# Sharing rows between VectorE and TensorE anew, and moving zero-writes, on the way back of a two-layer decode block

## The chip, the core and the metric

The kernel runs on one core of one Trainium2 chip. The metric is the device time of one execution in microseconds (us), given as the median of several runs. Profiles come from one further execution, taken by the hardware profiler.

## The reference

One token (a row of D = 1024 values) passes through four blocks, A, B, A, B, each added to its input after a layer norm. A is attention of 32 heads over the last 4096 positions of a cache with 4 key/value heads; B is a two-layer perceptron of width F = 3584 with the activation h * tanh(softplus(h)). The same weights serve both layers. Wanted are the output and the gradients with respect to the input, the caches and all weights:

```python
def _A_ref(x, k_cache, v_cache, wq, wo):
    q = (x @ wq).reshape(B, Sq, Hq, Dh).transpose(0, 2, 1, 3)
    k = jnp.repeat(k_cache[:, :, Sk - W:, :], rep, axis=1)      # W = 4096 of Sk = 32768
    v = jnp.repeat(v_cache[:, :, Sk - W:, :], rep, axis=1)
    p = softmax(einsum("bhqd,bhkd->bhqk", q, k) * Dh ** -0.5)
    o = einsum("bhqk,bhkd->bhqd", p, v)
    return o.transpose(0, 2, 1, 3).reshape(B, Sq, Hq * Dh) @ wo
def _B_ref(x, w1, b1, w2):
    h = x @ w1 + b1
    return (h * tanh(softplus(h))) @ w2
x = A_x
for _ in range(2):
    x = x + _A_ref(layernorm(x), k_cache, v_cache, wq, wo)
    x = x + _B_ref(layernorm(x), w1, b1, w2)
out, vjp = jax.vjp(f, A_x, k_cache, v_cache, wq, wo, w1, b1, w2)
return (out, *vjp(grad_out))
```

Only the last 4096 of 32768 positions of the caches have a gradient; the other seven eighths of both cache gradients are zeros, and they have to be written: 56 pieces of 1 MiB.

## The kernel before

**Work.** All is bf16, one token wide, so nearly everything is a matrix times a vector. Weights come in chunks of 1 MiB. The way forward goes through A0, B0, A1, B1; the way back through B1, A1, B0, A0; then the weight gradients, outer products of rows kept from both layers, are formed in PSUM (with a K of 2 or 32), copied to SBUF as bf16 and stored.

**Loads.** `Ring` has 8 slots. All loads stand in one list in the order of their use and go out on SyncE's queue; the next goes out when a slot is released (`release` calls `pump`, L68), which happens when the last reader of a chunk is done. Three chunks of wq (`KEEP_Q2`) stay in the ring between layer 1 and layer 0 of the way back, already turned. VS, KT and w1 have places of their own.

**Zeros.** `zeros(n, after)` takes the next n of the 56 pieces and issues them on GpSimd's queue (L248). If `after` is given, a copy of one element of that tile stands ahead of them (L243), so that they go out when the tile is there. The calls are placed by hand all along the program.

**The way back.** A gradient g is needed against the weights' other side, so a chunk's products can be made in two ways. VectorE takes a row of 1024 (`rowdot`, L422): it multiplies it with the gradient, broadcast over the partitions in PSUM (`bcast`, L325), and sums. Or TensorE turns eight blocks of 128 (`turned`, L445), ScalarE or VectorE copies them back over the ring slot (`evac_t`, L298 or L301, picked by a tally `load` of each engine's planned time), and TensorE multiplies them with the gradient's columns (`mv`, L457). These products are held back behind some later transposes (`later`, `behind`). In `attn_bwd` the tables `NR_O[l][c]` and `NR_Q[t]` say how many of a chunk's four rows go to VectorE; the rest is TensorE's. The w2 loop for layer 0 (L1103) gives two of four to each, and beside that TensorE finishes the forward product of layer 1 with the same chunk (`mlp_out`, L667).

In order of time after the forward pass: dh1; `dn_b1` (w1, resident) gives g3; `attn_bwd(1, ...)`: the wo loop (hook `do`, with pieces of KT and VS turned beside it by `conv`, L596), the softmax's way back (L868 to L900, hook `dp`), the wq loop (hooks `dq` and `dn`), and `ln_bwd` (L386) gives g2; the w2 loop gives dh0; `dn_b0` (L821) gives g1; `attn_bwd(0, ...)` gives g0; then `work` forms what is left of the weight gradients. `ln_bwd` calls its argument `beside` twice, ahead of and behind the matmul at L401; layer 0 passes `units_a0` there, layer 1 nothing.

**w1's last blocks.** `dn_b1` turns most of w1 in place. Blocks 4 to 7 of each of the eight parts are turned later, by `w1_rest` (L777, transposes at L783), since `dn_b0` reads them turned: two in hook `dp`, two in `dq`, four in `dn`.

**PSUM** has eight banks: SC (two, also LB, the broadcast rows), MV, TP, three BIG that transposes go through, and one that is free.

Of the kernel before, what the change touches and what calls it, by code (L numbers as in the profile page):

```python
# [83 lines left out]
def kernel(  # L84
# [65 lines left out]

    SC = [psum.tile([P, 512], FP32, name=f"SC{i}")[:] for i in range(2)]
    MV = psum.tile([P, 512], FP32, name="MV")
    TP = psum.tile([P, 512], FP32, name="TP")
    bigs = [psum.tile([P, 512], FP32, name=f"BIG{i}")[:] for i in range(3)]
    big_n = [0]
# [119 lines left out]
    def even():  # L275
        load["D"] = load["A"] = max(load.values())
# [138 lines left out]
    def rowdot(w, vecs, n, acc, fours=False):  # L415

        for i, vec in enumerate(vecs):
            out, a = junk[:, 0:n], w[:, i * n:(i + 1) * n]
            if fours:
                out, vec = (x.rearrange("a (k p) -> a k p", p=P) for x in (out, vec))  # L420
                a = a.rearrange("a (p k) -> a k p", k=4)
            nc.vector.tensor_tensor_reduce(out=out, in0=a, in1=vec, scale=1.0,  # L422
                                           scalar=acc if i else 0.0, op0=ALU.mult, op1=ALU.add, accum_out=acc)
        load["D"] += len(vecs) * (n * 1.1e-3 + 0.18)
# [4 lines left out]
    def later(f, product=False):  # L429

        lag.append((product, f))
        while sum(p for p, _ in lag) > behind[0]:
            lag.popleft()[1]()
        while lag and not lag[0][0]:
            lag.popleft()[1]()
# [5 lines left out]
    def turned(w, n, mv, eng=None, block=None):  # L441

        b = big().bitcast(BF16)
        for i in range(n):
            nc.tensor.transpose(b[:, i * P:(i + 1) * P], block(w, i) if block else w[:, i * P:(i + 1) * P], ident_bf[:])  # L445
        evac_t(w, b[:, 0:n * P], eng)
        later(mv, True)

    fresh = [False]

# [385 lines left out]

    NR_O = {1: (0, 3, 3, 3, 2, 2, 2, 2), 0: (0, 2, 2, 2, 2, 2, 2, 2)}
    NR_Q = (0, 2, 2, 2, 2, 1, 1, 1)  # L840

    def attn_bwd(l, sv, g, wo_key, wq_key, wq_keep, hooks, beside=None):
        name = f"A{l}"
        nc.vector.tensor_copy(GA[:, :, l], g[:])
        bcast(lambda c: GA[:, c, l:l + 1], TD)
        do32 = tmp([P, HQ], FP32, "da")
        mv_open()
        even()
        for c in range(8):
            ch = ring.get((*wo_key, c))  # L850

            behind[0] = max(2, 6 - c)
            rows_chunk(ch, c, GA, l, LB[0], do32, DA, NR_O[l][c], None)
            later(lambda c=c: ring.release((*wo_key, c)))
            hooks["do"](c)
        flush()
        x = 0
        while x < 8:
            k0, n0 = NR_O[l][x], x
            while n0 < 8 and NR_O[l][n0] == k0:  # L860
                n0 += 1
            nc.vector.tensor_copy(do32[:, 4 * x:4 * n0].rearrange("p (c k) -> p c k", k=4)[:, :, k0:],
                                  TP[:, DA + 4 * x:DA + 4 * n0].rearrange("p (c k) -> p c k", k=4)[:, :, k0:])
            x = n0
        do_n = from_fours(do32[:])
        dov = DOC[:].rearrange("p v (g u l h) -> p v g u l h", g=G, u=2, l=2)
        do4 = do_n.rearrange("p (g h) -> p g h", g=G)
        nc.vector.tensor_copy(dov[:, 0, :, 0, l, :], do4)  # L868
        nc.gpsimd.tensor_copy(dov[:, 1, :, 1, l, :], dov[:, 0, :, 0, l, :])
        pr = small[:, 64:128]  # L870
        prv = pr[:].rearrange("p (g u h) -> p g u h", g=G, u=2)
        o4 = sv["o32"][:].rearrange("p (g h) -> p g h", g=G)
        for u in range(2):
            nc.vector.scalar_tensor_tensor(out=prv[:, :, u, :], in0=do4, scalar=float(D), in1=o4, op0=ALU.mult, op1=ALU.mult)
        sdp = small[:, 224:288]
        pxv = PX[:].rearrange("p (b l h) -> p b l h", l=2, h=8)
        dsv = DSX[:].rearrange("p (b l h) -> p b l h", l=2, h=8)
        for i in range(2):
            for t in range(16 * i, 16 * i + 16):
                for g_ in range(G):  # L880
                    c = scol(g_, t) - 512 * i
                    nc.tensor.matmul(SC[i][:, c:c + 8], lhsT=VS[:, g_, t, :],  # L882
                                     rhs=DOC[:, 0, g_ * 32 + l * 8:g_ * 32 + l * 8 + 8], start=True, stop=True)
            if i == 0:
                nc.tensor.matmul(TP[:, 320:384], lhsT=onesD[:], rhs=pr[:], start=True, stop=True)
                nc.vector.tensor_copy(sdp[:], TP[:, 320:384])
            s = SC[i].rearrange("p (tp c) -> p tp c", c=64)
            nc.vector.tensor_tensor(out=s, in0=s, in1=sdp[:, None, :].to_broadcast([P, 8, 64]), op=ALU.subtract)
            nc.vector.tensor_tensor(out=dsv[:, i * 64:(i + 1) * 64, l, :], in0=SC[i].rearrange("p (b h) -> p b h", h=8),
                                    in1=pxv[:, i * 64:(i + 1) * 64, l, :], op=ALU.mult)  # L890
        even()
        hooks["dp"]()
        dq_ps = MV[:, 320:320 + HQ]
        for i in range(2):
            for g_ in range(G):
                for t in range(16 * i, 16 * i + 16):
                    c = pcol(g_, t, l)
                    nc.tensor.matmul(dq_ps[:, g_ * 8:g_ * 8 + 8], lhsT=KT[:, g_, t, :], rhs=DSX[:, c:c + 8],  # L898
                                     start=(g_ == 0 and t == 0), stop=(t == TS - 1), skip_group_check=True)
        nc.vector.tensor_scalar(out=DQC[:, :, l], in0=dq_ps, scalar1=scale, scalar2=None, op0=ALU.mult)  # L900
        bcast(lambda c: DQC[:, c, l:l + 1], TD)
        even()
        hooks["dq"]()
        mv_open()
        nc.vector.memset(dnp[:, 0:1], 0.0)
        for t in range(TD):
            key = (*wq_key, t)
            ch = ring.get(key)
            nr = NR_Q[t]
            behind[0] = max(2, 6 - t)  # L910
            if nr:
                rowdot(ch[:, 0:nr * D], LB[0:nr], D, dnp[:, t:t + 1])
            for k in range(nr, 4):
                h0 = 8 * k
                w = ch[:, h0 * P:(h0 + 8) * P]
                f = lambda w=w, h0=h0, t=t, k=k: mv(w, 8, TP[:, t:t + 1], lambda i: DQC[:, h0 + i, l:l + 1], k == 3)
                if key in turned_q:
                    later(f, True)
                else:
                    turned(w, 8, f)  # L920
            if t == 0:
                bcast(lambda c: DQC[:, c, l:l + 1], 2 * TD, None, TD)
            if t in wq_keep:
                ring.keep(key, ("q", 3, t))
                turned_q.add(("q", 3, t))
            else:
                later(lambda key=key: ring.release(key))
            hooks["dn"](t)
        flush()
        return ln_bwd(dnp, sv["n32"], sv["rstd"], g, name, beside)  # L930
# [3 lines left out]

    nc.vector.tensor_tensor(out=dh1[:], in0=da1[:, 0:TF], in1=mp1[:], op=ALU.mult)
    nc.vector.tensor_copy(DHC[:, :, 1], dh1[:])
    zeros(8, dh1)
    g3 = dn_b1(g4)
    sB1["act_late"]()
    put_by("AC", AC, TF)  # L940
    zeros(4, g3)

    def dp3():
        w1_rest(2)
        zeros(4)

    def dq3():
        w1_rest(2)
        zeros(3, DQC[:, 0, 1:2])

    def dn3(t):
        if t % 2:
            w1_rest(1)
        if t == 5:
            zeros(1, dnp[:, t:t + 1])

    assert all(NR_Q[t] == (1 if t in KEEP_Q2 else 2) for t in range(1, 8))
    g2 = attn_bwd(1, sA1, g3, ("o", 1), ("q", 2), KEEP_Q2,
                  dict(do=lambda c: conv(2), dp=dp3, dq=dq3, dn=dn3))


    W1S = W1[:].rearrange("p t f -> p (t f)")
# [131 lines left out]


    nc.vector.tensor_copy(GB[:, :, 0], g2[:])
    zeros(3, g2)
    bcast(lambda c: GB[:, c, 0:1], TD)
    da0 = tmp([P, HQ], FP32, "da")
    y_ps = MV[:, 384:384 + TD]  # L1100
# [2 lines left out]
    for c in range(7):  # L1103
        ch = ring.get(("2", 1, c))
        mlp_out(1, ch, c, y_ps)
        rows_chunk(ch, c, GB, 0, LB[0], da0, DA)
        later(lambda c=c: ring.release(("2", 1, c)))
    flush()
    rows_join(da0, TF, DA)
    nc.vector.tensor_tensor(out=dh0[:], in0=da0[:, 0:TF], in1=mp0[:], op=ALU.mult)  # L1110
    nc.vector.tensor_copy(DHC[:, :, 0], dh0[:])
    w1_rest(len(w1_units))
    zeros(2, dh0)
    g1 = dn_b0(g2)
    nc.vector.tensor_copy(GA[:, :, 0], g1[:])
    zeros(2, g1)

    x4 = sb([P, TD], BF16, "x4")
    nc.vector.tensor_tensor(out=x4[:], in0=y_ps, in1=x3[:], op=ALU.add)
# [41 lines left out]
        work(4)  # L1161

    g0 = attn_bwd(0, sA0, g1, ("o", 3), ("q", 3), (), dict(do=do1, dp=dp1, dq=dq1, dn=dn1), units_a0)
    g0b = sb([P, TD], BF16, "g0b")
    nc.vector.tensor_copy(g0b[:], g0[:])
    store_rows(g0b[:], TD, out_1[0, 0, :])
# [46 lines left out]
```

## Time and profile before

| | |
|---|---|
| median of 3 runs | 459.95 us (458.6 to 460.88) |
| the profiled execution | 460.51 us, of which span 458.4 us |
| TensorE (matmul) busy | 315.7 us, 69% |
| VectorE busy | 262.3 us, 57% |
| ScalarE busy | 185.6 us, 40% |
| DMA | 183.53 MB, mean 400 GB/s |
| loads and stores (queue q1) | 123.94 MB |
| zeros (queue q0) | 58.72 MB |

Stages of the way back in the profiled execution, in us from the start of the span: dh1 at 167.3, g3 at 187.5, wo loop of layer 1 to 215, its wq loop from 226 to 247.8, g2 at 249.6, w2 loop to 280.2, dh0 at 280.7, g1 at 292.3, layer 0's wo loop to 315.6 and wq loop to 346, then stores to 458.4.

How to read the profile: the span is cut into 40 slices of 11.5 us; each digit is a busy share in tenths, PEclk the granted TensorE clock, GB/s what the DMA engines moved. Tables of windows give, for a stretch from A to B, busy time and number of instructions of each engine (PE TensorE's matmuls, PEld its weight loads, DVE VectorE, ACT ScalarE, POOL GpSimd), then the granted clock, the DMA engines' busy share and GB/s. A timeline line has start, duration, engine, line of the kernel, operation, output<-input, shape and count; brackets hold the idle time before it and what ended it. A queue's line has packets, MB and its share of 16 engines' time.

### The profile page before, as it was taken

To read this page: it belongs to the slowest core of one execution; us is meant where nothing else is said; L and a number is where in the kernel's file an instruction comes from. 1 tells how busy PE (TensorE), PEld (TensorE's weight loads), DVE (VectorE), ACT (ScalarE), POOL (GpSimd) and SP (SyncE) were. 2 spreads that over 40 slices of the span, in tenths; PEclk is the share of its full clock that TensorE was granted. 3 is DMA by queue.
4 is the path that set the end of the run, shared out by engine and by line. 5 is a ranking of instruction groups with operands and counts; after the bars stand their busy time and mean duration, and the time that the engine had idled before them with its cause. 6 is when DMAs were issued, how large, how long until landed. Compare 5 with 4: busy or idle time off the path is not lost. (4 is left out here: it accounts for less than half of the span.)

```text
span 458.4 us, 13440 instructions
## 1 busy us (share of the span) xinstructions
PE 315.7 (69%) x5965; PEld 257.1 (56%) x5965; DVE 262.3 (57%) x514; ACT 185.6 (40%) x288; POOL 38.4 (8%) x85
## 2 busy tenths in 40 slices
PE   3836435597678799791797858667964776667870
PEld 3835434496668799691796857567861121122440
DVE  7305731283060148498378746397396987878770
ACT  2402001034032358390064321152255987888770
POOL 4000000000102321101202001102111000000000
PEclk9955555555555569795588555595585555555555
DMA  8999999999999999999999998879999999999996
GB/s 336 422 420 420 419 419 417 420 402 345 401 422 425 420 416 415 412 401 424 414 422 422 420 398 277 365 270 406 423 421 423 419 424 425 423 424 419 407 409 250
DMA packets 28375, 183.53 MB, mean 400 GB/s; under 512 B 3706, under 2 KB 3734, under 8 KB 9494
## 3 DMA queue, kind: packets, MB, share of 16 engines
q1 hardware_dynamic: 20162, 123.94, 66.5%
q0 software_dynamic: 8064, 58.72, 30.9%
q8 instruction: 46, 0.75, 0.6%
q14 instruction: 11, 0.09, 0.1%
q10 hardware_dynamic: 92, 0.02, 0.0%
HBM read 83.94 MB, written 98.62 MB: 398 GB/s over the span
## 5 line engine op out<-in xcount | busy, mean ns | idle before, releaser
L422 DVE CUSTOM_DVE_ANT_0 junk<-ring,SC 128x1024 bf16<-128x1024 bf16 x59 | 72.0, 1220 | 13.1 <-DMA ring<-in_B_w_dram 10.3
L301 ACT COPY ring<-BIG 128x512 f32<-128x512 f32 x82 | 47.7, 586 | 63.5 <-PE BIG L445 56.0
L445 PE MATMUL BIG<-ident_bf,ring 128*128 128x128 bf16 x720 | 69.8, 262 | 3.9 <-DMA ring<-in_A_wo_dram 3.6
L1021 PE MATMUL wide<-W 2*128 2x512 bf16 x228 | 48.9, 603 | 19.3 <-DVE VS L284 4.9
L445 PEld LDWEIGHTS <-ring 128*128 128x128 bf16 x720 | 56.5, 119 | 4.8 <-DMA ring<-in_A_wo_dram 4.0
L1021 PEld LDWEIGHTS <-W 2*128 2x128 bf16 x240 | 10.4, 103 | 52.2 <-issue 51.5
L284 DVE CAST ring<-wide 128x1024 bf16<-128x1024 f32 x27 | 31.6, 1217 | 6.4 <-PE wide L1021 3.8
L287 ACT CAST ring<-wide 128x1024 bf16<-128x1024 f32 (+1 forms) x37 | 33.6, 986 | 4.0 <-PE wide L1021 3.6
L457 PEld LDWEIGHTS <-ring 128*128 128x128 bf16 x792 | 30.3, 102 | 2.7 <-ACT ring L301 2.7
L248 POOL DMA_DIRECT2D out_dram<-zt x56 | 29.6, 534 | 7.2 <-DMA out_dram<-zt 6.4
L301 ACT COPY KT<-BIG 128x512 f32<-128x512 f32 x25 | 14.2, 584 | 38.8 <-PE BIG L596 35.6
L567 PE MATMUL MV<-OC,ring 128*128 128x1 bf16 x512 | 16.6, 166 | 15.0 <-DMA ring<-in_A_wo_dram 12.4
L567 PEld LDWEIGHTS <-ring 128*128 128x128 bf16 x512 | 16.0, 105 | 15.8 <-DMA ring<-in_A_wo_dram 13.0
L487 PE MATMUL MV<-NA,ring 128*128 128x1 bf16 x512 | 15.2, 165 | 12.5 <-DMA ring<-in_A_wq_dram 12.5
L301 ACT COPY W<-BIG 128x512 f32<-128x512 f32 (+1 forms) x29 | 13.5, 495 | 25.3 <-PE BIG L783 23.2
L615 PE MATMUL MV<-NB,W 128*128 128x1 bf16 x448 | 16.3, 172 | 9.3 <-DMA W<-in_B_w_dram 6.5
L422 DVE CUSTOM_DVE_ANT_0 junk<-ring,DSX 128x1024 bf16<-128x1024 bf16 x18 | 22.0, 1224 | 0.6
L284 DVE CAST VS<-wide 128x1024 bf16<-128x1024 f32 (+1 forms) x17 | 19.7, 1186 | 4.4 <-PE wide L1021 4.3
L487 PEld LDWEIGHTS <-ring 128*128 128x128 bf16 x512 | 14.4, 103 | 13.3 <-DMA ring<-in_A_wq_dram 13.3
L615 PEld LDWEIGHTS <-W 128*128 128x128 bf16 x448 | 16.0, 118 | 10.0 <-DMA W<-in_B_w_dram 7.6
L1072 PE MATMUL wide<-W 32*128 32x256 bf16 x128 | 20.6, 405 | 0.4 <-ACT VS L287 0.3
L667 PE MATMUL MV<-AC,ring 128*128 128x1 bf16 x448 | 13.8, 165 | 9.7 <-DMA ring<-in_B_w_dram 7.3
(252 smaller groups left out, 508.0 us busy)
## 6 DMA issues: line engine op xcount, KB each, us to landing
out_dram<-zt POOLq DMA_DIRECT2D x56, 1024.0 KB, 15.4
ring<-in_A_wq_dram SPq DMA_DIRECT2D x27, 1024.0 KB
ring<-in_A_wo_dram SPq DMA_DIRECT2D x24, 1024.0 KB
ring<-in_B_w_dram SPq DMA_DIRECT2D x14, 1024.0 KB
out_dram<-ring SPq DMA_DIRECT2D x9, 1024.0 KB
W<-in_B_w_dram SPq DMA_DIRECT2D x8, 896.0 KB
ring<-in_A_k_cache_dram SPq DMA_DIRECT2D x4, 1024.0 KB
VS<-in_A_v_cache_dram SPq DMA_DIRECT2D x4, 1024.0 KB
```

Source lines behind the costliest of these rows:

```text
L248: nc.gpsimd.dma_start(dst, zt[:])
L284: nc.vector.tensor_copy(dst, src)
L287: nc.scalar.copy(dst, src)
L301: nc.scalar.copy(dst.bitcast(FP32), src.bitcast(FP32))
L422: nc.vector.tensor_tensor_reduce(out=out, in0=a, in1=vec, scale=1.0, scalar=acc if i else 0.0, op0=ALU.mult, op1=ALU.add, accum_out=acc)
L445: nc.tensor.transpose(b[:, i * P:(i + 1) * P], block(w, i) if block else w[:, i * P:(i + 1) * P], ident_bf[:])
L457: nc.tensor.matmul(out, lhsT=w[:, i * P:(i + 1) * P], rhs=rhs_of(i), start=fresh[0], stop=last and i == n - 1, skip_group_check=True)
L487: nc.tensor.matmul(q_ps[:, h:h + 1], lhsT=ch[:, h * P:(h + 1) * P], rhs=NA[:, t, l:l + 1], start=(t == 0 and h == 0), stop=(t == TD - 1), ...
L567: nc.tensor.matmul(y_ps[:, dd:dd + 1], lhsT=ch[:, tt, dd * P:(dd + 1) * P], rhs=OC[:, h, l:l + 1], start=(h == 0 and dd == 0), stop=(h == ...
L615: nc.tensor.matmul(h_ps[:, fb:fb + 1], lhsT=f_block(W1[:, t], fb), rhs=NB[:, t, l:l + 1], start=(t == 0 and fb == 0), stop=(t == TD - 1), ...
L1021: nc.tensor.matmul(b[:, 512 * i:512 * i + 512], lhsT=R[at:at + 2, lo:lo + P], rhs=R[at:at + 2, ro + 512 * i:ro + 512 * i + 512], start=Tru ...
L1072: nc.tensor.matmul(b[:, k * 256:(k + 1) * 256], lhsT=RT[32 * g:32 * g + 32, a, tp, :], rhs=YS[32 * g:32 * g + 32, :], start=True, stop=Tru ...
```

## The change

- The tables: in the wo loops VectorE takes 14 rows instead of 17 (layer 1) and 12 instead of 14 (layer 0), in the wq loops 12 instead of 11 (layer 1) and 10 instead of 11 (layer 0). The first chunk, which TensorE had alone, now has one row for VectorE in all four; `NR_Q` gets a table for each layer, and the memset of `dnp` goes.
- w1's last blocks are turned in `rest_a1`, which layer 1 hands to `ln_bwd` as `beside`: three ahead of the matmul at L401, five behind it, with the copies steered to ScalarE.
- `warm(n)`: n matmuls of 128x512 of zeros into the free bank WM, which nobody reads; one in each chunk of the w2 loop.
- Zeros: with dh1 5 instead of 8, with g3 2 instead of 4, in `dp` 3 instead of 4, in `dq` 1 instead of 3, in layer 1's `dn` none instead of 1, with g2 none instead of 3, with dh0 3 instead of 2, with g1 3 instead of 2. The ten that are then left are issued with g0.

```diff
--- before.py
+++ after.py
@@ -150,6 +150,7 @@
 
     SC = [psum.tile([P, 512], FP32, name=f"SC{i}")[:] for i in range(2)]
     MV = psum.tile([P, 512], FP32, name="MV")
+    WM = psum.tile([P, 512], FP32, name="WM")
     TP = psum.tile([P, 512], FP32, name="TP")
     bigs = [psum.tile([P, 512], FP32, name=f"BIG{i}")[:] for i in range(3)]
     big_n = [0]
@@ -445,6 +446,11 @@
             nc.tensor.transpose(b[:, i * P:(i + 1) * P], block(w, i) if block else w[:, i * P:(i + 1) * P], ident_bf[:])
         evac_t(w, b[:, 0:n * P], eng)
         later(mv, True)
+
+    def warm(n):
+
+        for _ in range(n):
+            nc.tensor.matmul(WM[:], lhsT=ident_bf[:], rhs=zt[:, 0:512], start=True, stop=True)
 
     fresh = [False]
 
@@ -836,8 +842,8 @@
 
 
 
-    NR_O = {1: (0, 3, 3, 3, 2, 2, 2, 2), 0: (0, 2, 2, 2, 2, 2, 2, 2)}
-    NR_Q = (0, 2, 2, 2, 2, 1, 1, 1)
+    NR_O = {1: (1, 2, 2, 2, 2, 2, 2, 1), 0: (1, 1, 1, 2, 2, 2, 2, 1)}
+    NR_Q = {1: (1, 2, 2, 2, 2, 1, 1, 1), 0: (1, 2, 1, 2, 1, 1, 1, 1)}
 
     def attn_bwd(l, sv, g, wo_key, wq_key, wq_keep, hooks, beside=None):
         name = f"A{l}"
@@ -902,14 +908,12 @@
         even()
         hooks["dq"]()
         mv_open()
-        nc.vector.memset(dnp[:, 0:1], 0.0)
         for t in range(TD):
             key = (*wq_key, t)
             ch = ring.get(key)
-            nr = NR_Q[t]
+            nr = NR_Q[l][t]
             behind[0] = max(2, 6 - t)
-            if nr:
-                rowdot(ch[:, 0:nr * D], LB[0:nr], D, dnp[:, t:t + 1])
+            rowdot(ch[:, 0:nr * D], LB[0:nr], D, dnp[:, t:t + 1])
             for k in range(nr, 4):
                 h0 = 8 * k
                 w = ch[:, h0 * P:(h0 + 8) * P]
@@ -934,29 +938,27 @@
 
     nc.vector.tensor_tensor(out=dh1[:], in0=da1[:, 0:TF], in1=mp1[:], op=ALU.mult)
     nc.vector.tensor_copy(DHC[:, :, 1], dh1[:])
-    zeros(8, dh1)
+    zeros(5, dh1)
     g3 = dn_b1(g4)
     sB1["act_late"]()
     put_by("AC", AC, TF)
-    zeros(4, g3)
+    zeros(2, g3)
 
     def dp3():
-        w1_rest(2)
-        zeros(4)
+        zeros(3)
 
     def dq3():
-        w1_rest(2)
-        zeros(3, DQC[:, 0, 1:2])
-
-    def dn3(t):
-        if t % 2:
-            w1_rest(1)
-        if t == 5:
-            zeros(1, dnp[:, t:t + 1])
-
-    assert all(NR_Q[t] == (1 if t in KEEP_Q2 else 2) for t in range(1, 8))
+        zeros(1, DQC[:, 0, 1:2])
+
+    def rest_a1():
+
+        even()
+        load["D"] += 10
+        w1_rest(3 if len(w1_units) == TD else TD)
+
+    assert all(NR_Q[l][t] == 1 for l in range(2) for t in KEEP_Q2)
     g2 = attn_bwd(1, sA1, g3, ("o", 1), ("q", 2), KEEP_Q2,
-                  dict(do=lambda c: conv(2), dp=dp3, dq=dq3, dn=dn3))
+                  dict(do=lambda c: conv(2), dp=dp3, dq=dq3, dn=lambda t: None), rest_a1)
 
 
     W1S = W1[:].rearrange("p t f -> p (t f)")
@@ -1094,7 +1096,6 @@
 
 
     nc.vector.tensor_copy(GB[:, :, 0], g2[:])
-    zeros(3, g2)
     bcast(lambda c: GB[:, c, 0:1], TD)
     da0 = tmp([P, HQ], FP32, "da")
     y_ps = MV[:, 384:384 + TD]
@@ -1103,17 +1104,17 @@
     for c in range(7):
         ch = ring.get(("2", 1, c))
         mlp_out(1, ch, c, y_ps)
+        warm(1)
         rows_chunk(ch, c, GB, 0, LB[0], da0, DA)
         later(lambda c=c: ring.release(("2", 1, c)))
     flush()
     rows_join(da0, TF, DA)
     nc.vector.tensor_tensor(out=dh0[:], in0=da0[:, 0:TF], in1=mp0[:], op=ALU.mult)
     nc.vector.tensor_copy(DHC[:, :, 0], dh0[:])
-    w1_rest(len(w1_units))
-    zeros(2, dh0)
+    zeros(3, dh0)
     g1 = dn_b0(g2)
     nc.vector.tensor_copy(GA[:, :, 0], g1[:])
-    zeros(2, g1)
+    zeros(3, g1)
 
     x4 = sb([P, TD], BF16, "x4")
     nc.vector.tensor_tensor(out=x4[:], in0=y_ps, in1=x3[:], op=ALU.add)
@@ -1161,6 +1162,7 @@
         work(4)
 
     g0 = attn_bwd(0, sA0, g1, ("o", 3), ("q", 3), (), dict(do=do1, dp=dp1, dq=dq1, dn=dn1), units_a0)
+    zeros(len(zjobs), g0)
     g0b = sb([P, TD], BF16, "g0b")
     nc.vector.tensor_copy(g0b[:], g0[:])
     store_rows(g0b[:], TD, out_1[0, 0, :])
```

## Prediction

> **What bounds the kernel now.** I read the page first (the 40 slices, the queues), then the table of windows by stage, the queues' bytes in chosen stretches, and the timelines of the engines.
>
> ```profile
> span 458.4 us, 13440 instructions
> ...
> PEclk9955555555555569795588555595585555555555
> DMA  8999999999999999999999998879999999999996
> GB/s 336 422 420 420 419 419 417 420 402 345 401 422 425 420 416 415 412 401 424 414 422 422 420 398 277 365 270 406 423 421 423 419 424 425 423 424 419 407 409 250
> ...
> HBM read 83.94 MB, written 98.62 MB: 398 GB/s over the span
> ```
>
> No engine is full, the transfers are: 0.42 MB per us in nearly every slice. 183.53 MB (the page's packets line) at 0.420 take 437 us of the 458.4. The change moves no byte more or less, so the time is 437 us plus whatever the queues lose. Where they lose after the first touched instruction (167.4):
>
> ```profile
> core 0: us, PE busy (x) PEld busy (x) DVE busy (x) ACT busy (x) POOL busy (x), PEclk, DMA share, GB/s
> ...
> 187.50:216.00 28.50, 19.07 (x365) 18.62 (x366) 23.61 (x45) 14.15 (x27) 2.24 (x5) 0.80 1.01 410
> 226.00:249.70 23.70, 19.00 (x378) 18.46 (x378) 16.75 (x35) 12.47 (x24) 2.51 (x7) 0.86 1.01 421
> 249.70:281.00 31.30, 22.81 (x458) 22.32 (x459) 17.84 (x32) 8.19 (x14) 1.97 (x6) 0.50 0.93 375
> 281.00:292.50 11.50, 7.67 (x207) 7.08 (x207) 6.93 (x27) 1.26 (x2) 1.12 (x3) 0.50 0.93 358
> 292.50:316.00 23.50, 17.78 (x302) 16.80 (x303) 19.10 (x36) 10.34 (x19) 1.78 (x5) 0.72 0.84 321
> ...
> 350.00:458.40 108.40, 70.63 (x392) 24.34 (x391) 76.97 (x67) 79.38 (x89) 0.00 (x0) 0.50 0.97 401
> ```
>
> 249.7 to 316 moved 31.3x375 + 11.5x358 + 23.5x321 = 23.4 MB, which is 55.7 us of work in 66.3: **10.6 us lost**. That is all that this change can win back, and what it may add to. The next views say why the way there is long:
>
> ```profile
> 206.22 0.35 PE L457 MATMUL TP<-GA,ring 128*128 128x1 bf16 x8 [0.21 <-ACT ring L301]
> 215.49 0.27 PE L352 MATMUL TP<-junk,spread 128*128 128x32 bf16 x4 [8.92 <-DVE junk L348]
> ```
> ```profile
> 266.12 1.22 DVE L422 CUSTOM_DVE_ANT_0 junk<-ring,SC 128x1024 bf16<-128x1024 bf16 x1 [2.58 <-DMA ring<-in_B_w_dram]
> ...
> 271.17 1.22 DVE L422 CUSTOM_DVE_ANT_0 junk<-ring,SC 128x1024 bf16<-128x1024 bf16 x1 [2.56 <-DMA ring<-in_B_w_dram]
> ```
>
> In layer 1's wo loop TensorE has finished at 206.6 and waits for VectorE's rows. In the w2 loop both wait 2.6 us per chunk for a load, because each load shares the engines with zeros. And the zeros queued ahead of it:
>
> ```profile
> q0 software_dynamic: 1801, 13.19, 68.0%
> q1 hardware_dynamic: 946, 6.05, 32.3%
> ```
>
> (queues, 121 to 167.4): of the 15 MiB of zeros issued by then, 15.73 MB, 13.19 have gone and 2.5 are left.
>
> **The change, part by part.** Durations: a VectorE row comes every 1.26 us; turning a row on TensorE is 0.445 for 8 transposes and 0.20 for 8 products at full clock, 0.80 and 0.26 at half; a ScalarE copy 0.61 (1.22 for two).
>
> *Layer 1, wo loop: 17 rows on VectorE become 14, one in the first chunk.* VectorE starts at 189.0 instead of 193.5 and needs 14x1.26 + one copy = 18.3: to 207.3. TensorE: 18 rows x 0.645 + 14 pieces of the caches x 0.445 = 17.8, broadcast 0.85, and 2.0 more while the clock is 0.50: to 208.5. ScalarE: 31 copies x 0.61 from 189.8: 208.7, with waits about 209.5; then the last products: 210.2 against 215.0: **-4.8** (-7.3 if only VectorE bound, -3 if TensorE and ScalarE keep waiting on each other).
>
> *The w1 units* (L783) leave the path ahead of L898 and of the first wq chunk: 0.82 of transposes once (**-0.8**), the other pair with the next item. Beside the norm three fit into TensorE's 1.7 us wait at L401 (3 x 0.23); the other five, paced by 0.42 copies on idle ScalarE, hold back the broadcast of GB behind them: **+0.4** (0 to 0.8).
>
> *Layer 1, wq loop: 12 rows on VectorE instead of 11, from the first chunk on.* Before, four rows are turned first and VectorE starts at 233.5, ends at 247.7. Now it starts when the broadcast is done (228.8 on the old time, TensorE's 1.6 us "issue" stop kept), loses about 1 at the second broadcast: 228.8 + 15.1 + 1.0 = 245.1: **-2.5** (-4.5 without stop and wait, -1 if TensorE's 20 rows at 0.645 with a cold start end later).
>
> *w2 loop.* Seven zeros fewer stand ahead of these loads (dp 3 for 4, dq 1 for 3, wq 0 for 1, g2 0 for 3; 4 issued, were 11). Five of the seven chunks are then in before the loop starts, and what is late next is VectorE: 14 x 1.26 = 17.7 after a broadcast of 0.45, 0.2 more at the end: 18.4 against 30.3 (249.85 to 280.2): **-11.9**. That holds while TensorE needs under 2.53 a chunk: 32 products 0.80, two rows 1.30, the new 512-column matmul 0.23 (four transposes' worth) = 2.33 at full clock. At half clock it is 0.87 + 2.12 + 0.43 = 3.42, the loop about 25.7 and the gain -4.6: the other end.
>
> So g1 comes at 292.3 - 4.8 - 0.8 - 2.5 + 0.4 - 11.9 = **272.7**. dn_b0 between them (11.5 us) is unchanged.
>
> *The zeros.* By g1 the kernel used to issue 40, now 29, and g1's own three. What can move ahead of g1's: 2.5 MB left, 14 zeros (5+2+3+1+3) and 20 loads (8 wq, 7 w2, 5 wo): 2.5 + 34x1.0486 = 38.2 MB = 91.0 us. With no gap they'd be through at 167.4 + 91.0 = 258.4. g1's zeros flow at about 274.0 (1.1 us after issue at 292.6, where others had just gone; about 4 after 280.9, on an idle queue). So **15.6 us** are lost. Where: 186 to 190 (five zeros drained, g3's two still to come) 4; 195 to 197 until the first wo slot is free, 2; 227 to 229.5 until the first wq slot, 2.5; 242 to 247 until the first w2 slot (five ring slots filled, no zeros at g2), 5; the small row copies and g1, 2.
>
> *Layer 0's loops* (12 rows for 14, 10 for 11, about -5 and -4 us by the same terms) are worth nothing: from g1 on the queue is full. g1's three zeros last 7.5 us, to 281.5, and the first wo slot comes free about 8 us after g1 (300.4 against 292.4 before), so it fits to a us; behind it stand 8 loads, 14 zeros, the ten left over at g0, and the stores. These ten wait on POOL for g0 with nothing behind them. Cover gone would be copies out of PSUM becoming the bound, but these need 156 us on two engines, 78 each, and g0, at 272.7 + 54.2 less 4 to 9 = 318 to 323, leaves 135. The lost memset (0.06) and the third copy at L862 (0.1) vanish there too.
>
> **Sum.** 15.6 lost instead of 10.6: +5.0. On the profiled execution (span 458.4 and 2.1 around it, 460.5) 465.5. It lies 0.55 above the median of 459.95, so 465.0 for the median.
>
> **Rivals.** *The clock drops in the w2 loop* (slower still). For: at 250 to 259 TensorE is busy throughout and granted 0.50. Against: the clock went to 1.00 at 233 and stayed to 249 with two thirds of the time in transposes, and now units and broadcast fill the pause in which it fell (0.67 in 249 to 250), and the 512-column matmul raises the share of moving columns. Dropped for the whole loop +7.4, dropped halfway +3.7: 468.7 to 472.4. The Trainium skill ("TensorE: Matmul & The Clock Gate", Part 4: PE-mode transpose) says that full clock "doesn't engage" for transposes, so by that rule only the added matmul would count and the loop would be cold throughout, 472.4. The trace disagrees: full clock in 233 to 249.
>
> *A wash*: the loops get down to VectorE's bare sums (wo -7.3, wq -4.5). Then g1 is at 268.2, 11.1 us are lost, +0.5: 460.5, with a us or two less if stops of the "issue" kind shrink.
>
> *Faster: the bound is the slowest of the 16 DMA engines, not the mean.* At the end of long zeros one trails:
>
> ```profile
> q1 hardware_dynamic: 635, 4.64, 84.8%
> q0 software_dynamic: 126, 0.86, 16.0%
> ```
>
> (204 to 217): 0.86 MB in 13 us, by the end (212 to 217, the packets of q0) a trickle of 0.015 MB per us, half of one engine's 0.026. Half of 13 us is 6.5 of one engine's work behind the rest. If the end waits for that engine, gaps in which the others rest cost it up to 6.5 less: 465.0 - 6.5 = 458.5, and with the wash's g1 454. It decides where the last packets come from one engine for over 6 us; the last slice's 250 GB/s allows at most 4.6, so I hold it for less likely.
>
> *The shorter loops do not come about*: if the loads came as late as before and g1 stayed at 292.3, its zeros would flow at 293.6 and 293.6 - 258.4 = 35 us be lost instead of 10.6: 485. Against: loads alone run at 0.42 (slices 4 to 8 of the page).
>
> **Chances.** Forecast 0.44 (461.5 to 468), clock 0.16, late loads 0.02, wash 0.20, slow engine 0.18. A measurement of this kernel can tell about 0.5%, 2.3 us, from no change: 457.65 to 462.25. Faster: 0.13 of the slow engine and 0.06 of the wash (shorter stops) = 0.19. Within: 0.05 and 0.14 of these and 0.02 of the forecast's low edge = 0.21. Slower: 0.42 + 0.16 + 0.02 = 0.60. Range 456 to 471: left out are half of the slow engine's case below, half of the clock's and the late loads above, 0.09 + 0.08 + 0.02.
>
> **What would show it.** Right: DVE waits for no ring load in the w2 loop and its clock is 1.00; g1 near 273; GB/s dips near 188, 196, 228 and 244; no dip from 281 to the end, g0 near 323. A loop at 0.50 points to the clock; no dips before 245 would make the sum wrong at its base, and a last stage at less than 0.42 would mean that the postponed zeros are not neutral.

## The result, and the profile after

The changed kernel takes **464.27 us** (median of 20 runs, 460.35 to 468.16) against 459.86 for the kernel before (20 runs, 457.83 to 460.88): a ratio of 1.0091, 95% interval 1.0069 to 1.0114. It is slower, by some 4.4 us or 0.9%; 465.0 was forecast. The profiled execution took 468.16 us, the slowest of the 20, so below its profile says where time is lost, and the medians say how much. Being more than 1.5% above the fastest it counts as a slow run, and the ratio leaves it out.

The page of the changed kernel, with the span, the granted clock and the DMA engines in 40 slices of 11.7 us:

```profile
span 466.4 us, 13602 instructions
...
PEclk9955555555555569797896559758555555555555
DMA  8999999999999999499997899999999999999996
GB/s 338 421 419 420 420 416 419 419 393 367 399 423 422 406 409 408 197 334 406 421 379 280 310 413 406 400 422 422 421 420 415 423 422 419 419 419 416 410 409 259
```

Before, the GB/s row sagged in one place, 275 to 309 us (277, 365 and 270 GB/s). That sag is gone; in its place there are two, slices 17 and 18 (187 to 210) and 21 to 23 (233 to 268). The last slices are as they were (409 and 259 for 409 and 250), although ten zeros more now go out in layer 0. The windows by stage (us; busy time of PE, PEld, DVE, ACT and POOL; granted clock, DMA share, GB/s):

```profile
184.00:204.00 20.00, 17.50 (x327) 17.29 (x325) 12.97 (x31) 12.90 (x26) 1.24 (x3) 0.83 0.64 236
204.00:243.00 39.00, 33.85 (x836) 32.96 (x835) 28.67 (x61) 20.01 (x40) 2.51 (x6) 0.87 1.01 416
243.00:264.00 21.00, 18.94 (x425) 18.47 (x428) 16.57 (x30) 8.11 (x14) 0.89 (x3) 0.64 0.77 281
264.00:275.00 11.00, 7.05 (x198) 6.45 (x195) 7.00 (x28) 1.26 (x2) 1.12 (x4) 0.50 0.97 369
275.00:350.00 75.00, 60.06 (x985) 42.35 (x986) 52.76 (x87) 43.23 (x68) 14.45 (x32) 0.68 1.01 415
```

A stretch loses its length times the shortfall from 420 GB/s as a share of 420. So 184 to 204 loses 20 x (420 - 236)/420 = 8.8 us, 243 to 264 loses 7.0 and 264 to 275 another 1.3. From g1 (274.7) on nothing to speak of is lost. Finer windows show how dry the queues are (a queue is dry when it has little or nothing to move), with TensorE and VectorE busy nearly throughout:

```profile
196.00:200.00 4.00, 4.00 (x98) 4.00 (x96) 3.86 (x8) 3.85 (x8) 0.00 (x0) 1.00 0.30 47
...
244.00:248.00 4.00, 3.92 (x111) 3.76 (x109) 3.90 (x8) 1.95 (x5) 0.00 (x0) 1.00 0.32 74
```

The loops did get shorter: from g3 to g1 it takes 85.4 us (189.3 to 274.7) where it took 104.8. No row of the w2 loop waits for a ring load any more. That time went back into the queues: they empty before the next zeros come.

One line for each of the two kernels over the same 180 us, 165 to 345, gives a single number, first before, then after:

```profile
165.00:345.00 180.00, 136.57 (x2910) 130.74 (x2908) 122.27 (x269) 70.98 (x135) 22.35 (x51) 0.70 0.97 394
```
```profile
165.00:345.00 180.00, 151.31 (x3064) 133.54 (x3069) 128.18 (x276) 95.46 (x174) 21.97 (x50) 0.75 0.94 377
```

Lost there: 180 x (420 - 394)/420 = 11.1 us before, 18.4 after. The span less this loss is 447.3 before and 448.0 after: outside these 180 us hardly anything changed. This pair of numbers is the measure in the experiments. It is bookkeeping: it says where the time is lost, and the kernels with zeros or loops altered say why.

### The profile page after: what moved, and what is told of

It reads as the page before. It is cut to its first block, busy times and chain, and to the rows that moved or that the text cites. A ratio compares the mean times of both kernels' runs of the same rounds, so it can differ in the third digit from the quotient of the medians.

```text
span 466.4 us, 13602 instructions
## 1 busy us (share of the span) xinstructions
PE 314.3 (67%) x6046; PEld 256.2 (55%) x6052; DVE 251.2 (54%) x494; ACT 191.9 (41%) x302; POOL 38.4 (8%) x84
## 5 line engine op out<-in xcount | busy, mean ns | idle before, releaser
L302 ACT COPY ring<-BIG 128x512 f32<-128x512 f32 x94 | 54.2, 588 | 59.7 <-PE BIG L446 56.9
L423 DVE CUSTOM_DVE_ANT_0 junk<-ring,SC 128x1024 bf16<-128x1024 bf16 x56 | 68.3, 1220 | 9.3 <-PE SC L326 5.4
L446 PE MATMUL BIG<-ident_bf,ring 128*128 128x128 bf16 x760 | 68.4, 250 | 5.1 <-DMA ring<-in_A_wo_dram 3.7
L573 PE MATMUL MV<-OC,ring 128*128 128x1 bf16 x512 | 16.6, 166 | 15.8 <-DMA ring<-in_A_wo_dram 12.6
L493 PE MATMUL MV<-NA,ring 128*128 128x1 bf16 x512 | 15.1, 165 | 13.4 <-DMA ring<-in_A_wq_dram 13.4
L493 PEld LDWEIGHTS <-ring 128*128 128x128 bf16 x512 | 14.3, 103 | 14.1 <-DMA ring<-in_A_wq_dram 14.1
L288 ACT CAST KT<-wide 128x1024 bf16<-128x1024 f32 (+1 forms) x20 | 19.5, 1009 | 1.8 <-PE wide L1023 1.6
L1074 PEld LDWEIGHTS <-W 32*128 32x128 bf16 x128 | 11.6, 123 | 10.5 <-issue 6.8
## 6 DMA issues: line engine op xcount, KB each, us to landing
out_dram<-zt POOLq DMA_DIRECT2D x56, 1024.0 KB, 15.1
```

The lines of the kernel that those rows point to most:

```text
L288: nc.scalar.copy(dst, src)
L302: nc.scalar.copy(dst.bitcast(FP32), src.bitcast(FP32))
L493: nc.tensor.matmul(q_ps[:, h:h + 1], lhsT=ch[:, h * P:(h + 1) * P], rhs=NA[:, t, l:l + 1], start=(t == 0 and h == 0), stop=(t == TD - 1), ...
L573: nc.tensor.matmul(y_ps[:, dd:dd + 1], lhsT=ch[:, tt, dd * P:(dd + 1) * P], rhs=OC[:, h, l:l + 1], start=(h == 0 and dd == 0), stop=(h == ...
L1074: nc.tensor.matmul(b[:, k * 256:(k + 1) * 256], lhsT=RT[32 * g:32 * g + 32, a, tp, :], rhs=YS[32 * g:32 * g + 32, :], start=True, stop=Tru ...
```

## The experiments

**Theory**: the time is 437 us of transfers plus what the queues lose by running dry; the shorter loops count only through that, and moving zeros behind g0 emptied the queues where the loops had become short. **Rivals**: the new rows and turns cost time themselves; the postponed zeros do (slowest DMA engine, or a last stage too full); the clock in the w2 loop does.

| kernel | median us | ratio to before (95%) | span of the profile | GB/s in 165 to 345 | lost there | span less lost |
|---|---|---|---|---|---|---|
| before | 459.86 | 1 | 458.4 | 394 | 11.1 | 447.3 |
| changed | 464.27 | 1.0091 (1.0069 to 1.0114) | 466.4 | 377 | 18.4 | 448.0 |
| changed, zeros as before | 458.4 | 0.9967 (0.9947 to 0.9986) | 457.3 | 397 | 9.9 | 447.4 |
| before, zeros as changed | 476.82 | 1.0358 (1.0312 to 1.0403) | 476.7 | 352 | 29.1 | 447.6 |
| changed, old row tables | 474.2 | 1.0296 (1.026 to 1.0333) | 472.5 | 362 | 24.9 | 447.6 |
| changed, old tables in layer 0 | 463.42 | 1.0069 (1.0043 to 1.0094) | 460.4 | 389 | 13.3 | 447.1 |
| changed, no warm | 462.08 | 1.0052 (1.0024 to 1.008) | 460.6 | 389 | 13.3 | 447.3 |
| changed, warm(2) | 461.44 | 1.0045 (1.0021 to 1.0069) | 460.5 | 391 | 12.4 | 448.1 |
| changed, 2 more with dh1 | 457.61 | 0.9964 (0.9939 to 0.9988) | 455.6 | 402 | 7.7 | 447.9 |
| changed, 3 with g2 | 459.73 | 0.9995 (0.9962 to 1.0028) | 461.7 | 387 | 14.1 | 447.6 |
| changed, both of these | **457.04** | 0.9938 (0.9917 to 0.996) | 454.8 | 406 | 6.0 | 448.8 |
| both, and warm(2) | 457.29 | 0.9952 (0.9913 to 0.999) | 454.2 | 407 | 5.6 | 448.6 |
| both, and 2 more | 457.75 | 0.9961 (0.9944 to 0.9978) | 456.0 | 402 | 7.7 | 448.3 |
| changed, 5 of the last ten with dp of layer 0 | 463.86 | 1.0112 (1.0075 to 1.015) | 458.5 | 389 | 13.3 | 445.2 |

Single executions, and so the spans, lie up to 4 us off the medians; the last column hardly moves.

**Rows and zeros, each alone.** The changed kernel with the zeros where they were:

```
zeros(8, dh1); zeros(4, g3); dp: zeros(4); dq: zeros(3, DQC[:, 0, 1:2])
dn: zeros(1, dnp[:, t:t + 1]) if t == 5; zeros(3, g2); zeros(2, dh0); zeros(2, g1)
```

> The row tables, w1's last blocks and the added matmul of the change, with the zeros of before (8, 4, 4, 3, 1, 3, 2, 2 and none left for g0). Theory (the time is 437 us plus what the queues lose; shorter loops only let them run dry earlier): 45 pieces of zeros and loads, 25 + 20, stand ahead of g1's zeros again, about 118 us of transfers after dh1, so the w2 loop waits for its loads as before (about 2.5 us a chunk), g1 comes at 288 to 291 and not at 273, 8 to 10 us are lost: 457 to 460.5 us, no change or 0.5% faster. Rival (the chain of compute to g1 sets the time): 19 us of shorter loops show, 441 to 450.

458.4: the rows, turns and added matmuls cost nothing by themselves, and bring 1.5 us of what they could. VectorE's timeline in its w2 loop (bracket: idle time and what ended it) says why:

```profile
260.15 1.22 DVE L423 CUSTOM_DVE_ANT_0 junk<-ring,SC 128x1024 bf16<-128x1024 bf16 x1 [2.52 <-DMA ring<-in_B_w_dram]
...
265.20 1.22 DVE L423 CUSTOM_DVE_ANT_0 junk<-ring,SC 128x1024 bf16<-128x1024 bf16 x1 [2.56 <-DMA ring<-in_B_w_dram]
```

The loads come every 5 us as before, since zeros share the engines with them. The loop waits for full queues, which costs nothing but gains nothing.

The other half, the kernel before with nothing but the zeros moved:

```
zeros(5, dh1); zeros(2, g3); dp: zeros(3); dq: zeros(1, DQC[:, 0, 1:2]); dn: -
g2: -; zeros(3, dh0); zeros(3, g1); after g0: zeros(len(zjobs), g0)
```

> The kernel before with the zeros of the change alone (5, 2, 3, 1, 0, 0, 3, 3, ten with g0); rows, w1's last blocks as before, no added matmul. Theory: the same 38 MB ahead of g1's zeros as in the change (91 us), but g1 only about 8 us earlier than before (the w2 loop no longer waits for loads, at half clock it takes 23 us): g1 near 285, 27 us lost, 474 to 479 us. Rival (zeros slow the loads, and the fewer the better): faster than before, 452 to 456.

476.82, and its windows show a hole in each of the three loops (184 to 204 has 261):

```profile
226.00:249.00 23.00, 19.30 (x396) 18.87 (x393) 16.01 (x31) 12.44 (x24) 0.72 (x2) 0.84 0.69 270
249.00:274.00 25.00, 22.65 (x461) 22.40 (x461) 18.77 (x37) 8.19 (x14) 0.35 (x2) 0.53 0.71 265
```

So the zeros' new places cost 476.82 - 459.86 = 17.0 us on the old loops and 464.27 - 458.4 = 5.9 on the new ones; everything else together is worth 12.6 us with the new places and 1.5 with the old. One number for "the rows" doesn't exist: a loop's length counts where the queue is dry at its end.

**Which rows.** The changed kernel with the old tables in both layers, and with the old tables in layer 0 alone:

```
NR_O = {1: (0, 3, 3, 3, 2, 2, 2, 2), 0: (0, 2, 2, 2, 2, 2, 2, 2)}     # second kernel: entry 1 as changed
NR_Q = {l: (0, 2, 2, 2, 2, 1, 1, 1) for l in range(2)}                # second kernel: entry 1 as changed
memset of dnp back; rowdot only if nr
```

> The change with the row tables of before in both layers (and the memset that they need); its zeros, w1's last blocks and added matmul stay. Theory: layer 1's wo loop takes 4.8 us longer, its wq loop 2.5 us, g1 comes 7 us later with the same transfers ahead of it, so 7 us more are lost: 469 to 473 us. Rival (the rows buy nothing, the time is set by the bytes behind g1): 463 to 466, as the change.

> The change with the row tables of before in layer 0's loops alone. Theory: from g1 on the queue is full, so 9 us of loops more or less in layer 0 move nothing: within 1.5 us of the change, 463 to 466 us (up to 2 us more if the first wo slot comes free later, since four rows are turned first and g1's zeros last only 7.5 us). Rival (the loops of layer 0 are on the path): 470 to 474.

474.2 and 463.42. Layer 1's tables are worth some 10 us with these zeros; layer 0's nothing that shows (intervals 1.0043 to 1.0094 and 1.0069 to 1.0114 overlap), which fits a queue that is full from g1 on. The first came 1.2 us above its range; what the old loops cost beyond the sums for them wasn't resolved.

**The clock.** Without `warm(1)`, and with two such matmuls in each chunk:

> The change without the 512-column matmul in the w2 loop. In the change's profile the granted clock fell from 1.00 to 0.50 after three of seven chunks with it. Theory: at half clock a chunk takes TensorE 3.0 instead of 3.4 us, at full clock 2.1 instead of 2.3; if the clock falls a chunk or two earlier the loop ends within 1 us of the change's, 463 to 466 us. Rival (the matmul holds the clock): the loop is at half clock from its start and 3 to 5 us longer, 467 to 470.

> The change with two 512-column matmuls in each chunk of the w2 loop. Theory (the clock falls when too small a share of a window's time goes into moving columns; one matmul gave about 0.4 of it, two give 0.5): the clock stays at 1.00 through the loop, a chunk takes TensorE 2.55 us, the loop 18.5 instead of 21.5, g1 3 us earlier, 3 us less lost: 460 to 462.5 us. Rival (the clock falls all the same after three chunks): 3.85 us a chunk at half clock, the loop 23 us, 465 to 467.

Taking it out made the kernel no slower (462.08, below the range given), two gave 461.44. Windows of the w2 loop, first without any, then with two, then with one, the last from the profile of the control below, whose instructions are the changed kernel's up to g1:

```profile
246.00:248.00 2.00, 2.00 (x66) 2.00 (x63) 1.93 (x5) 1.17 (x2) 0.00 (x0) 0.97 1.03 373
248.00:250.00 2.00, 2.00 (x47) 2.00 (x46) 1.97 (x3) 1.03 (x2) 0.00 (x0) 0.50 1.05 348
```
```profile
240.00:244.00 4.00, 4.00 (x108) 3.52 (x106) 3.90 (x7) 2.16 (x4) 0.00 (x0) 1.00 0.11 27
...
252.00:256.00 4.00, 3.80 (x100) 3.40 (x96) 3.85 (x8) 2.22 (x4) 0.00 (x0) 1.00 1.00 391
```
```profile
236.00:256.00 20.00, 18.14 (x480) 16.91 (x477) 18.52 (x35) 9.60 (x19) 0.17 (x1) 1.00 0.82 319
```

Without any the clock falls at 248; with two it holds to the loop's end. With one it goes both ways: in the changed kernel's profile it falls at 249, in the control's it holds to the end, as it does in the version below with two more zeros with dh1. So these runs do not show that the share of moving columns decides it, as the theory had it. From g2's cast to the end of the rows the loop takes 18.7 us without the matmul, 19.1 with two, and with one 21.7 where the clock fell and 18.4 where it held. Without the matmul a chunk takes TensorE 2.1 us at full clock, less than VectorE's 2.53, so it is ahead when the clock falls; that this is why the fall cost that loop so little is argued, not shown.

What the cold part of the loop costs the changed kernel isn't settled: 464.27 - 461.44 = 2.8 us lie between one matmul and two, but 0.6 between none and two. Nor is it the whole of its loss: with the clock held, the queue still stands at 27 GB/s in 240 to 244, and the kernel is still slower than before (1.0021 to 1.0069).

**Filling the holes.** Five of the ten zeros that were left for g0 go back to where the two holes begin: two with dh1, three with g2; each alone, then both:

```
-    zeros(5, dh1)          nc.vector.tensor_copy(GB[:, :, 0], g2[:])
+    zeros(7, dh1)        + zeros(3, g2)
```

> The change with two more zeros with dh1 (7 for 5), eight left for g0. Theory: they fill 5 us of the 8 to 9 lost between 184 and 204 and delay no load, as the first wo slot comes free only at about 196: 5 us less, 458 to 461 us. Rival (zeros ahead of the wq loads push these back and with them the wq loop): 463 to 465.

> The change with three more zeros with g2 (3 for 0), seven left for g0. Theory: between 243 and 264 8 us are lost, of which three zeros, 7.5 us, fill 4 to 6, since the loads of the second half of the w2 loop would have come in the rest: 458.5 to 461 us. Rival (the w2 loop's last two loads come later and stretch it): 463 to 466.

> The change with two more pieces of zeros with dh1 (7 for 5) and three with g2 (3 for 0), so that five and not ten are left for g0. Theory: 5.2 MB fill 12.5 us of the times in which the queues ran dry (186 to 200, 243 to 264) and move no loop by more than 1 us; g1 at 273 to 276, some 5 us lost: 452 to 458 us. Rival (zeros beside the loads delay the w2 loop, which sets the time): the loop takes 6 us longer and nothing is won, 463 to 467.

457.61 (a little better than its range), 459.73 (its profiled execution, 463.52, was the slowest of its ten) and 457.04. The last is faster than both kernels: 0.9938 (0.9917 to 0.996) of before, and 7.2 us below the changed one with the same instructions on TensorE, VectorE and ScalarE. Its page and windows:

```profile
DMA  8999999999999999999999999999999999999995
GB/s 335 421 421 420 417 422 414 420 412 340 393 424 421 418 419 415 417 373 408 423 385 398 411 353 422 404 413 421 420 421 420 421 424 419 421 422 414 410 408 203
```
```profile
184.00:204.00 20.00, 17.55 (x328) 17.26 (x328) 14.61 (x28) 13.56 (x26) 1.24 (x3) 0.83 0.98 392
...
243.00:264.00 21.00, 17.79 (x381) 16.36 (x379) 14.78 (x28) 7.03 (x12) 0.83 (x3) 0.64 0.99 391
```

236 has become 392 and 281 has become 391, in the same windows and at the same clocks. The w2 loop took 23.6 us in this profile, 1.9 more than in the changed kernel's (with a 1.51 us stop of TensorE in it and a load awaited for 0.66), where 1 had been allowed; no lost transfers show for it. The gains are not additive (6.7 and 4.5 alone, 7.2 together). That bytes ahead of g1 buy nothing more once the queue is nearly full up to there is the likely reason; it was not tested by itself.

**Is a full queue the end of it?** On top of both, `warm(2)`; and on top of both, one more with g3 and in `dq` each, with three left for g0:

> Both: five more zeros (two with dh1, three with g2) and two 512-column matmuls in each chunk. Theory: of the 5.5 us still lost there after dh1, the earlier g1 wins 2 to 3: 454 to 456 us. Rival (with the queue full g1 no longer matters): 456.5 to 457.5, as with the zeros alone.

> The version with two more at dh1 and three at g2, and one more each with g3 (3 for 2) and in layer 1's dq (2 for 1); three left for g0. Theory: of the 5.5 us lost there after dh1 1.2 lie at 195 to 210 and 0.9 at 225 to 240, the rest are small copies and unequal ends; at most 2 us to win, at worst the loads come a us later: 455 to 457.5 us. Rival (each zero moved ahead of g0 wins 2.5 us): 450 to 453.

457.29 and 457.75: no gain, the second 0.25 above its range. For the first the rival's range won; I had taken 2 to 3 us for an earlier g1. Its profile doesn't quite test that, though: a stop of TensorE cost it the clock for one stretch of the loop (last section), and g1 came only 1.0 us earlier than with the fills alone (273.2 for 274.2). So `warm(2)` wins nothing there; that an earlier g1 is worth nothing behind a full queue fits, but isn't shown.

**A control.** Five of g0's ten moved earlier too, but to a place where the queue is full, `dp` of layer 0 (`zeros(9)` for `zeros(4)`):

> The change with five of the ten zeros of g0 issued some 25 us earlier, in layer 0's dp (9 for 4), where nothing is lost. It moves as many zeros ahead of g0 as the version with two more at dh1 and three at g2. Theory: only the place counts, the queue is full there, so nothing changes: 462.5 to 466 us. Rival (zeros behind g0 are late and stretch the end, the earlier the better): 455 to 459.

463.86 (1.0075 to 1.015), as the changed kernel. Five zeros moved out of the last stage are worth nothing, five moved into the holes 7.2 us. So it is not the number of zeros behind g0 that costs. (Its span less the loss, 445.2, is the low one of the table: its first ten slices lost 3.0 us where before's lost 4.9 and the changed kernel's 4.7, ahead of all that differs.)

## Why the prediction came out right, point by point

**The base of the sum** held: 437 us and what the queues lose. In fourteen kernels from 457 to 477 us the span less the loss in 165 to 345 is 447.1 to 448.8 but for the one just named. What is left over 437 is the start and the last slice: before lost 4.9 us in its first ten slices and 4.9 in its last two.

**The loss ahead of g1's zeros**: 15.6 forecast; from 168.5 to 275 the windows give 17.8, in an execution 3.9 us above its median. Of the four dips named, 188, 196 and 244 are there; at 228 there is none (422 GB/s in 228 to 232), and 252 to 264 has one that I didn't name (289 to 332 in 4 us windows).

**The loops**: in the profiled execution g3 to g1 is 19.4 us shorter, 19.6 was forecast, but by terms that erred both ways:

| | forecast | measured |
|---|---|---|
| wo loop | -4.8 | -5.6 (27.4 to 21.8) |
| w1 units off the path to the wq loop | -0.8 | 0: a 2.07 us "issue" stop of TensorE at 220.9 takes it |
| wq loop | -2.5 | -5.1 (21.7 to 16.6): the 1.6 us stop kept in the sum didn't recur, the second broadcast cost 0.1 and not 1 |
| units beside the norm | +0.4 | 0: the broadcast of GB started 0.06 after VectorE's cast had ended |
| w2 loop | -11.9 | -8.7 (30.4 to 21.7) |

(In the wq term 228.8 + 15.1 + 1.0 is 244.9, not 245.1; that is 0.2 of its error.) Two errors of about 3 us thus cancel, so that the closeness of 464.27 to 465.0 is in part luck: 2.6 us in the wq loop that weren't there, and 3.2 us in the w2 loop that were. The larger mis-sized step is the w2 loop, and its other end was written there: half clock. TensorE had full clock for three of the seven chunks and lost it at 249:

```profile
249.10 1.06 PE L446 MATMUL BIG<-ident_bf,ring 128*128 128x128 bf16 x8 [0.22 <-issue]
...
252.51 1.06 PE L446 MATMUL BIG<-ident_bf,ring 128*128 128x128 bf16 x8 [0.24 <-issue]
```

A chunk takes 3.41 us there, as the 3.42 worked out for half clock, instead of VectorE's 2.53. VectorE ends its rows at 259.4 and waits:

```profile
262.61 0.17 DVE L479 COPY da<-TP 128x14 f32<-128x14 f32 x1 [3.24 <-PE TP L463]
```

The slow chunks also hand back ring slots, and so call for loads, every 3.41 us: 1.0486 MB in that time is 307 GB/s, which is about the dip of 252 to 264.

The 3.2 us come and go. In the control's profile, with the same instructions up to g1, the clock held and the loop took 18.4 us, the sum's own figure; g3 to g1 took 82.3, 13.3 us were lost, and that execution took 460.25, the wash's figure (460.5). Of the changed kernel's 20 executions, the five fastest had a mean granted clock of 0.624 to 0.633 and the five slowest of 0.608 to 0.620, which fits, but only one of them was profiled, so in how many the clock fell in this loop isn't known.

**After g1**: as forecast. 285 to 300 lost 3.2 us before and 0.9 after; g0 came at 327 (318 to 323 forecast), late by the w2 loop and by a load awaited at 289.8, and this cost nothing.

**The rivals.** *Clock*: it came in the profiled execution, halfway through the loop, and the 3.3 us between 21.7 and 18.4 are near its price (+3.7 for a drop halfway); the stop and the broadcast that didn't come paid for it. In the control's profile it did not come. The Trainium skill ("TensorE: Matmul & The Clock Gate", Part 4: PE-mode transpose) has full clock not engage for transposes. The kernel without `warm` ran nothing but transposes and one-column products at 1.00 from 239 to 247, so the measurement decides against that as a general rule. *Wash*: in the profiled execution its wq loop came (-5.1 for -4.5), its wo loop (-5.6 for -7.3) and the w2 loop didn't; the median is 3.8 us above its 460.5. *Slowest DMA engine*: falls. It needed time lost before g1 not to count at the end; all of it counts, as the last column of the table of runs shows (but for the control it moves by 1.7 us while the loss goes from 5.6 to 29.1). *Late loads*: falls, no ring load is awaited in the w2 loop of the changed kernel. They come back with the old zeros, without harm.

## What to carry to other kernels

Where transfers bound the time, as here, write beside each point at which more can be issued the bytes queued ahead of it and the time to get there; where the bytes at the full rate take the shorter time, the difference is lost for good, and the busy shares of the compute engines don't show it. Writes that depend on nothing belong just ahead of such a stretch, in the amount that fills it: 2 and 3 MiB here won 7 us, and 5 MiB in a full queue nothing. Shorten a loop and place the fill together, since each is worth what the other leaves over (1.5 or 12.6 us for the same rows here).

## What the runs showed of the hardware beyond that

- Transposes with one-column products between them kept full clock, once it was there, for 8 us (239 to 247 without `warm`), and then lost it with TensorE still fully busy. With two 512-column matmuls (0.43 us the pair) in each 2.53 us they kept it to the end of the loop. With one they kept it in two profiles (the control's, and two more with dh1), and lost it in two others with no stop of TensorE ahead of that (the changed kernel's at 249, old tables in layer 0 at 246).
- Before, the clock's changes fell on a grid. Read from windows of half a us they lie at 167.4, 184.5, 191.3, 208.4, 232.3 and 249.3, that is 17.1, 6.8, 17.1, 23.9 and 17.0 us apart, or 5, 2, 5, 7 and 5 times 3.41. The Trainium skill ("TensorE: Matmul & The Clock Gate", Part 1) tells of a free-running window of about 3.4 us, and the trace agrees. That the place of a loop on this grid decides whether it loses its clock would account for the same instructions keeping and losing it; it was not tested.
- A stop of TensorE's sequencer ("issue") can cost the clock as well. In four profiles (3 with g2, both fills, both and `warm(2)`, both and 2 more) a stop of 1.5 to 2.3 us stands in the w2 loop, and the clock fell from 1.00 to 0.50 during it or within 1.5 us of its end. With both and `warm(2)` it fell at 251.9 and was back at 255.3. TensorE's timeline has the stop ahead of that:

```profile
250.45 0.21 PE L463 MATMUL TP<-GB,ring 128*128 128x1 bf16 x3 [1.89 <-issue]
```

- Kernels whose queue stays nearly full scatter less: both fills 456.45 to 457.92 (7 executions), with two more 457.31 to 458.52 (10), before 457.83 to 460.88 (20); the changed kernel 460.35 to 468.16 (20). That fits the account that what varies in the loops reaches the time only through a dry queue.
